# Sliding-window attention and sentence-level experts on one core: the fourth v in one transfer, the fifth v a step earlier, and a conversion behind an output copy

## The chip, the core and the metric

The kernel runs on one core of one Trainium2 chip, in one launch. The metric is the device time of that core in microseconds (us), as the median of the runs shown. The core has a matrix engine (TensorE, PE in the profile), a vector engine (VectorE, DVE), a scalar engine (ScalarE, ACT), a general engine (GpSimd, POOL) and a sync engine (SP) that issues transfers and computes nothing. POOL and SP each feed a queue of the same 16 DMA engines: POOL's queue (q0, "software") carries everything that is converted from float32 on the way, which is q, k and the experts' weights; SP's queue (q1, "hardware") carries v, unconverted, and the outputs.

## What is computed

```python
def _attn_ref(q, k, v):                      # (8, 8, 576, 64) each, float32
    ...
    mask = (rel >= 0) & (rel < window)       # window = 64
    scores = np.where(mask, scores, -1000000000.0)
    ...
    return np.matmul(attn, v)

def _moe_ref(x, w_gate, w1, w2):             # x: (8, 576, 512), the heads side by side
    logits = x.mean(axis=1) @ w_gate
    e_idx = np.argmax(logits, axis=1)        # one of 8 experts for a whole sentence
    ...
    gate_w = probs[np.arange(B), e_idx]
    h = np.maximum(x[mask] @ w1[e], 0.0)     # w1[e]: 512 x 1024
    out[mask] = gate_w[mask, None, None] * (h @ w2[e])   # w2[e]: 1024 x 512
```

Which weights a sentence needs is known only when its attention is finished, its mean is taken and its gate is computed. So the two megabytes of w1 and the two of w2 (float32; half that after conversion) of a sentence can be asked for no earlier than that.

## The kernel before

Eight sentences b of eight heads make 16 units u: unit u holds four heads of sentence u // 2. Of a unit, `load_qk` brings q and k (bf16), `transpose_qk` turns each on PE and ACT or DVE copies it out of PSUM (`leave_qk`), `scores` multiplies them in three chunks c with an exponential on ACT and a mask on DVE (`mask_out`), and `values` multiplies the result (`pt`) with v in two halves, after which DVE normalizes it into `x`. v of a whole sentence comes in one tile `vn` (128 x 36 x 64, float32, 1.2 MB) by `load_v`. `cast_v(u)` converts the half of it that unit u needs: three DVE instructions, one into `va` ("whole") and two from `va` into `vb` ("low" and "high", shifted by 64 rows). `transpose_x` turns x into `xT`, ACT sums it along the way, and `gate(b)` finds the expert. Then `load_w1` and `load_w2` bring its weights. `expert_up` is x times w1, in eight pieces ft (`php`, with the relu to `hT` on ACT), and `expert_down` is h times w2 in five pieces (`pso`; DVE or ACT copies each to an `ob` tile, and SP sends that out).

The order is written out by hand. A prologue brings units 0 to 3 on the way. Then comes a loop over steps t = 4, 5, ...; step t does the scores and values of unit t, and between them a stream of expert pieces (`experts(pace)`) of earlier sentences, to keep PE busy. In each even step `next_gate` computes a gate and asks for weights: sentence 1's at t = 4, sentence 2's at t = 6, and so on. `LAG`, `START = 3` and `per_step` set the pace.

Every PSUM tile comes from one pool of four (`tag="ps"`): a matrix product starts only when the tile it is given has been read out. `vpool` has three tiles, so v of sentence 3 takes the tile of sentence 0, and v of sentence 4 that of sentence 1. `opool` has ten output tiles, two sentences' worth. SP issues its transfers one after another in program order, each when what it waits for is there.

The transfers of v around the change are these. `load_v(2, ...)` is held by a one-element copy on POOL until the first half of sentence 0's w1 has landed. `load_v(3, part=20)` follows and brings 20 of 36 blocks. At the start of t = 5, `load_rest(3, 20, ...)` brings the other 16, held in the same way until the second half of sentence 1's w1 has landed. `load_v(4)` stands at the end of t = 5, and from t = 6 on `load_v` stands in `next_gate` behind `load_w2`.

w1 of sentences 0 and 1 comes in two halves (`w1_parts`), and each half serves four pieces ft: pieces 0 to 3 need the first, 4 to 7 the second.

Of the kernel before, what the change touches and what calls it, by code (L numbers as in the profile page):

```python
# [156 lines left out]
def kernel(  # L157
# [10 lines left out]
    nc = tc.nc  # L168
    B, H, S, D = q.shape
# [7 lines left out]
    NM = H * S // 128  # L177
    scale = 1.0 / float(D) ** 0.5

    def P(ins):  # L180
        tc.keep_in_program_order(ins)
        return ins
# [20 lines left out]
    vv = v.rearrange("b h s d -> b (h s) d").rearrange(  # L203
        "b (m p) d -> b p m d", p=128)
# [3 lines left out]
    def load_qk(u):  # L208
        qn = qkn.tile([128, 2, NT * D], BF16, tag="qn")
        kn = qkn.tile([128, 2, NT * D], BF16, tag="kn")  # L210
        P(nc.gpsimd.dma_start(out=qn, in_=qv[u]))
        if u == 0:
            load_v(0)
        P(nc.gpsimd.dma_start(out=kn, in_=kv[u]))
        qk_tiles[u] = (qn, kn)

    v_tiles = {}

    def load_v(b, behind=None, part=0):
        vn = vpool.tile([128, NM, D], FP32, tag="vn")  # L220
        if behind is None:

            P(nc.gpsimd.memset(vn[:, 0, 0:1], 0.0))
        else:

            P(nc.gpsimd.tensor_copy(out=vn[:, 0, 0:1], in_=behind))
        v_tiles[b] = vn
        if part:
            P(nc.sync.dma_start(out=vn[:, 0:part, :], in_=vv[b][:, 0:part, :]))
        else:  # L230
            P(nc.sync.dma_start(out=vn, in_=vv[b]))

    def load_rest(b, part, behind):
        vn = v_tiles[b]
        P(nc.gpsimd.tensor_copy(out=vn[:, part, 0:1], in_=behind))
        P(nc.sync.dma_start(out=vn[:, part:NM, :], in_=vv[b][:, part:NM, :]))

    HM = NM // 2

# [34 lines left out]
    for (half, e, own) in ((0, 0, True), (1, 0, False), (0, 1, False), (1, 1, True)):  # L274
        sl = par[64 * half:64 * half + 64, e, :]
        if own:

            P(nc.gpsimd.affine_select(
                out=sl, in_=sl, compare_op=ALU.is_ge, fill=OUT, base=0,
                pattern=[[1, 64]], channel_multiplier=-1))  # L280
        else:

            P(nc.gpsimd.affine_select(
                out=sl, in_=sl, compare_op=ALU.is_ge, fill=OUT, base=-1,
                pattern=[[-1, 64]], channel_multiplier=1))
    outside = const.tile([128, 3, 6, 64], BF16)
    for c in range(3):
        P(nc.vector.tensor_copy(
            out=outside[:, c].rearrange("p (g e) w -> p g e w", e=2),
            in_=par[:, None, :, :].broadcast_to([128, 3, 2, 64])))  # L290
# [22 lines left out]
    def cast_part(u, part, eng=None):  # L313
        b, qd = divmod(u, 2)
        i = b % 2
        vn = v_tiles[b]
        lo, hi = qd * HM, qd * HM + HM
        l1 = max(lo, 1)

        src = vn if eng is nc.gpsimd else va[i]  # L320
        eng = eng or nc.vector
        if part == "whole":
            copy_on(eng, va[i][:, lo:hi, 0:D], vn[:, lo:hi, :])
        elif part == "low":
            copy_on(eng, vb[i][0:64, lo:hi, 0:D], src[0:64, lo:hi, 0:D])
        else:
            copy_on(eng, vb[i][64:128, l1:hi, 0:D], src[64:128, l1 - 1:hi - 1, 0:D])

    def cast_v(u):
        for part in ("whole", "low", "high"):  # L330
            cast_part(u, part)
# [70 lines left out]
    def mask_out(u, c):  # L402
        pt = pt_tiles[u, c]
        P(nc.vector.tensor_tensor(  # L404
            out=pt, in0=pt, in1=masks[:, c].rearrange("p s g w -> p s (g w)"),
            op=ALU.mult))
# [92 lines left out]
    def gate(b):  # L499
        gl = psum.tile([128, 2, 512], FP32, tag="ps", name="gl")  # L500
        P(nc.tensor.matmul(out=gl[:, 0, 0:E], lhsT=onesf, rhs=gparts[b],  # L501
                           start=True, stop=True))

        glog = small.tile([128, E], FP32, tag="glog")
        P(nc.vector.tensor_copy(out=glog, in_=gl[:, 0, 0:E]))
        gmx = small.tile([128, 8], FP32, tag="gmx")
        P(nc.vector.max(out=gmx, in_=glog))
        graw = small.tile([128, 8], U32, tag="graw")
        P(nc.vector.max_index(out=graw, in_max=gmx, in_values=glog))
        P(nc.vector.tensor_scalar(out=eidx[:, b, :], in0=graw, scalar1=E - 1,  # L510
                                  scalar2=None, op0=ALU.min))
        gnm = small.tile([128, 1], FP32, tag="gnm")
        P(nc.vector.tensor_scalar(out=gnm, in0=gmx[:, 0:1], scalar1=-1.0 / S,
                                  scalar2=None, op0=ALU.mult))
        gate_in[b] = glog, gnm

        ereg = nc.gpsimd.alloc_register(f"er{b}")
        P(nc.gpsimd.load(ereg, eidx[0:1, b, 0:1]))
        experts_of[b] = ds(nc.gpsimd.snap(ereg, donate=True), 1)
        weights[b] = (wpool.tile([128, KB, F], FP16, tag="w1t", name=f"w1t{b}"),  # L520
                      wpool.tile([128, FB, Dm], FP16, tag="w2t", name=f"w2t{b}"))
# [13 lines left out]
    def w1_parts(b):  # L535
        return weights[b][0].rearrange("p k f -> p (k f)").rearrange(
            "p (h k f) -> p h k f", h=NQ, k=KB)

    def load_w1(b):
        if b < 2:  # L540

            src = w1c[experts_of[b]].squeeze(0)
            for hf in range(NQ):
                P(nc.gpsimd.dma_start(out=w1_parts(b)[:, hf],
                                      in_=src[:, :, ts(hf, F // NQ)]))
        else:
            P(nc.gpsimd.dma_start(  # L547
                out=weights[b][0].rearrange("p (g kl) f -> p g kl f", kl=2),
                in_=w1e[experts_of[b]].squeeze(0)))

    def load_w2(b):
        P(nc.gpsimd.dma_start(
            out=weights[b][1].rearrange("p (g i) d -> p g i d", i=4),
            in_=w2e[experts_of[b]].squeeze(0)))
# [102 lines left out]
    def experts(amount):  # L657

        acc[0] += amount
        while acc[0] > 0.0:  # L660
            nxt = next(stream, None)
            if nxt is None:
                return
            nxt[0]()
            halves[0] = False
            acc[0] -= nxt[1]

            free[0] = nxt[2]

    per_step = (8 * 1.0 + 4 * 1.7 + 0.9) / 2  # L670
    START = 3
# [73 lines left out]
    load_w2(0)  # L745
    load_qk(5)
    load_v(2, w1_parts(0)[:, 0, 0, 0:1])
    load_qk(6)
    load_v(3, part=20)
    for c in range(3):  # L750
        scores(2, c)
        if c == 0:
# [28 lines left out]
    for t in range(START + 1, NU + LAG):  # L781
        pace = per_step / 8.0 * 0.96
        on, prev, ahead = t < NU, START + 1 < t <= NU, t + 1 < NU

        def next_gate():
            b = t // 2 - 1
            gate(b)
            load_w1(b)
            if START + 1 < t < NU - 3:
                load_qk(t + 3)  # L790
            load_w2(b)
            if START + 1 < t and t // 2 + 2 < B:
                load_v(t // 2 + 2)
            if t == START + 1:
                load_qk(7)

        gated = START < t <= NU and t % 2 == 0
        if t % 2 == 1 and t + 3 < NU:
            load_qk(t + 3)
        if t == START + 2:  # L800

            load_rest(3, 20, w1_parts(1)[:, 1, 0, 0:1])
        if prev:
            transpose_x(t - 1)
        if ahead and t > 5 and not gated:
            cast_part(t + 1, "whole")
        if on:
            scores(t, 0, not gated)
            scores(t, 1, not gated)
        if t > START + 1:  # L810
            experts(pace)
        if gated:

            next_gate()
            if on:
                mask_out(t, 0)
                mask_out(t, 1)
        if t == START + 1:
            experts(pace)
        if t == NU:  # L820
            gate_weight(B - 1)
            okc = row_check()
        if ahead and t > 5:
            if gated:
                cast_part(t + 1, "whole")
        experts(pace)
        if on:
            scores(t, 2)
        if gated and on:
            gate_weight(t // 2 - 1)  # L830
        if ahead and t > 5:
            cast_part(t + 1, "low")
            cast_part(t + 1, "high")
        if t == START + 1:
            cast_v(t)
        experts(pace)
        experts(pace)

        if ahead:
            transpose_qk(t + 1, 1, leave=False)  # L840
            leave_qk(t + 1, 1, free[0])

        late = t == START + 1
        if late:
            transpose_qk(t + 1, 0)
        elif on:
            values(t, 0)
        halves[0] = on
        experts(pace)
        experts(pace)  # L850
        if ahead and not late:
            transpose_qk(t + 1, 0)
        if late:
            values(t, 0)
        if on:
            values(t, 1)
        halves[0] = on
        if t in (4, 5):
            cast_v(t + 1)
        if t == START + 2:  # L860
            load_v(4)
        if t == NU:
            row_flag(okc)
        experts(pace)
        experts(pace)
    experts(1e9)


# [35 lines left out]
```

## Time and profile before

| | |
|---|---|
| time, three runs | 225.25, 225.32 and 226.03 us; median 225.32 |
| profiled execution | 225.92 us; span from first to last instruction 224.0 us |
| granted TensorE clock, mean | 0.972 |
| busy in the span | PE 201.1 us (90%), ACT 134.2 (60%), DVE 128.6 (57%), POOL 39.1 (17%) |
| moved by DMA | 45.64 MB, 204 GB/s on average |
| POOL's queue, SP's queue | 26.22 MB and 18.75 MB |

Times in the profile are in us from the span's start. A row of a timeline has the start, the duration, the engine, the line, what was done, and in brackets how long the engine had been idle before and what it is taken to have waited for. Where several waits end together, one of them is named. A row of transfers gives how many, the size of one and the us from issue to landing; for v it shows 0.2 KB, the size of one piece, where the transfer is 1.2 MB. The chain of work is followed back from the last instruction to what released it.

### The profile page before, as it was taken

How to read it: one execution, taken by the hardware profiler on the slowest of the kernel's cores; microseconds unless marked ns; L12 is line 12 of the kernel's file. 1: busy time of each engine (PE TensorE's matmuls, PEld its weight loads, DVE VectorE, ACT ScalarE, POOL GpSimd, SP SyncE). 2: the span in 40 equal slices, each digit the busy share in tenths (PEclk: the TensorE clock that was granted, in tenths of full speed). 3: DMA queues.
4: the chain of work that ended last, by engine and by line, in shares of the span. 5: the costliest groups of instructions: out<-in, count | busy, mean ns of one | idle time of the engine just before them, and what ended most of it. 6: DMA issues, size and time to landing. Idle time of an engine off the chain costs nothing.

```text
span 224.0 us, 6996 instructions
## 1 busy us (share of the span) xinstructions
PE 201.1 (90%) x3012; PEld 141.4 (63%) x3012; DVE 128.6 (57%) x310; ACT 134.2 (60%) x221; POOL 39.1 (17%) x69
## 2 busy tenths in 40 slices
PE   7859759999799897999999999999999998999960
PEld 2437638856586556865696658775777567569520
DVE  2538696557866665576774769395939373330120
ACT  2275695964768464785769476968495656417300
POOL 7170161053000700034000700050002000200000
PEclk9976999999999999999999999999999999999995
DMA  5999899999999999999999999999956990699141
GB/s 69 243 256 246 149 157 219 242 251 235 257 225 203 236 223 244 230 288 217 244 227 277 218 231 235 250 264 219 246 141 113 212 266 5 97 225 263 52 136 41
DMA packets 34310, 45.64 MB, mean 204 GB/s; under 512 B 7136, under 2 KB 26720, under 8 KB 34272
## 3 DMA queue, kind: packets, MB, share of 16 engines
q0 software_dynamic: 14624, 26.22, 65.3%
q1 hardware_dynamic: 18704, 18.75, 28.9%
q8 instruction: 25, 0.41, 0.7%
q10 hardware_dynamic: 944, 0.16, 0.4%
q14 instruction: 13, 0.11, 0.1%
HBM read 61.90 MB, written 9.44 MB: 318 GB/s over the span
## 4 chain that ended last, share of the span: by engine, by line
PE 64%; DMA 12%; ACT 11%; DVE 6%; issue 2%; POOL 1%; POOLq 0%
PE php L570 26%; PE pso L584 20%; DMA w1t<-in_moe_w_dram 8%; PE tp L342 6%; ACT xT L470 5%; DMA kn<-in_k_dram 4%; PE op L425 4%; ACT hT L574 4%; PE sp L382 2%; PE pso L601 2%; ACT pt L397 2%; DVE x L441 1%; PE tp L462 1%; DVE vb L311 1%; PE gl L501 1%
## 5 line engine op out<-in xcount | busy, mean ns | idle before, releaser
L570 PE MATMUL php<-xT,w1t 128*128 128x288 f16 x512 | 70.0, 287 | 3.4 <-DMA w1t<-in_moe_w_dram 2.3
L574 ACT ACTIVATE hT<-php,gatew 128x576 f16<-128x576 f32 x64 | 47.2, 744 | 28.8 <-PE php L570 28.6
L570 PEld LDWEIGHTS <-w1t 128*128 128x128 f16 x512 | 56.0, 115 | 10.0 <-DMA w1t<-in_moe_w_dram 2.9
L584 PE MATMUL pso<-w2t,hT 128*128 128x512 f16 x256 | 60.2, 380 | 0.2
L397 ACT ACTIVATE pt<-sp 128x768 f16<-128x768 f32 x48 | 36.4, 817 | 7.5 <-PE sp L382 7.5
L584 PEld LDWEIGHTS <-hT 128*128 128x128 f16 x256 | 23.3, 98 | 26.1 <-issue 1.2
L311 DVE COPY ob<-pso 128x512 f32<-128x512 f32 x23 | 15.9, 690 | 22.9 <-PE pso L584 22.7
L441 DVE TENSOR_TENSOR x<-op,linv 128x640 f16<-128x640 f32 x32 | 26.4, 825 | 1.1
L404 DVE TENSOR_TENSOR pt<-pt,masks 128x768 f16<-128x768 f16 x42 | 22.6, 554 | 5.7 <-ACT pt L397 4.7
L355 ACT COPY dst<-tp 128x1152 bf16<-128x1152 bf16 x16 | 18.0, 1124 | 11.9 <-PE tp L342 11.7
L547 POOL DMA_DIRECT2D w1t<-in_moe_w_dram x6 | 4.4, 729 | 112.8 <-DVE pt L404 91.5
L470 ACT ACTIVATE xT<-tp 128x576 f16<-128x576 f16 x28 | 17.9, 646 | 9.2 <-PE tp L462 9.2
L425 PE MATMUL op<-vb,pt 128*64 128x65 f16 x320 | 16.2, 198 | 0.8 <-DVE ob L311 0.7
L311 DVE COPY vb<-va 64x1152 f16<-64x1152 f16 (+1 forms) x32 | 15.9, 498 | 0.5
L425 PEld LDWEIGHTS <-pt 128*64 128x64 f16 x640 | 13.9, 114 | 3.3 <-issue 2.4
L425 PE MATMUL op<-va,pt 128*64 128x65 f16 x320 | 15.9, 198 | 0.0
L382 PE MATMUL sp<-dst 64*64 64x128 bf16 (+1 forms) x672 | 14.2, 218 | 1.9 <-ACT dst L309 1.2
L382 PEld LDWEIGHTS <-dst 64*64 64x64 bf16 x672 | 10.3, 110 | 8.7 <-issue 4.5
L311 DVE CAST va<-vn 128x1152 f16<-128x1152 f32 x16 | 12.2, 763 | 6.2 <-DMA vn<-in_v_dram 6.1
L493 DVE SCALAR_TENSOR_TENSOR gpart<-wg,pooled,gpart 128x8 f32<-128x8 f32 x21 | 4.8, 226 | 18.4 <-ACT xT L470 18.1
L342 PE MATMUL tp<-ident,kn 128*64 128x128 bf16 x288 | 11.5, 227 | 1.9 <-DMA kn<-in_k_dram 1.9
L342 PEld LDWEIGHTS <-kn 128*64 128x64 bf16 x288 | 9.0, 113 | 6.0 <-issue 3.5
(74 smaller groups left out, 178.5 us busy)
## 6 DMA issues: line engine op xcount, KB each, us to landing
w2t<-in_moe_w_dram POOLq DMA_DIRECT2D x8, 1024.0 KB, 17.6
out_dram<-ob SPq DMA_DIRECT2D x31, 256.0 KB, 8.1
w1t<-in_moe_w_dram POOLq DMA_DIRECT2D x6, 1024.0 KB, 9.4
qn<-in_q_dram POOLq DMA_DIRECT2D x16, 288.0 KB, 13.2
kn<-in_k_dram POOLq DMA_DIRECT2D x16, 288.0 KB, 14.3
w1t<-in_moe_w_dram POOLq DMA_DIRECT2D x4, 512.0 KB, 8.3
out_dram<-ob SPq DMA_DIRECT2D x16, 64.0 KB, 7.3
vn<-in_v_dram SPq DMA_DIRECT2D x1, 640.0 KB, 21.1
```

What stands on the lines that cost most here:

```text
L311: P(eng.tensor_copy(out=out, in_=in_))
L342: P(nc.tensor.transpose(out=tp[64 * s:64 * s + 64, ts(t, 128)], in_=src[:, s, ts(t, D)], identity=ident, tile_position=(0, 64 * s)))
L355: P(nc.scalar.copy(out=dst.rearrange("p (x r t) -> p x r t", x=2, t=NT), in_=view))
L382: P(nc.tensor.matmul(out=sp[64 * half:64 * half + 64, s, 64 * (qblk - 6 * c):64 * (qblk - 6 * c) + n], lhsT=kT[64 * s:64 * s + 64, ts(kblk ...
L397: P(nc.scalar.activation(out=pt, in_=sp[:, :, 0:384], func=AF.Exp, scale=scale))
L404: P(nc.vector.tensor_tensor(out=pt, in0=pt, in1=masks[:, c].rearrange("p s g w -> p s (g w)"), op=ALU.mult))
L425: P(nc.tensor.matmul(out=op[64 * half:64 * half + 64, xx, 65 * jj:65 * jj + 65], lhsT=pt[:, s, 64 * (g % 6):64 * (g % 6) + 64], rhs=win, s ...
L441: P(nc.vector.tensor_tensor(out=x[:, :, h0 * D:(h0 + 2) * D].rearrange("p j (x c) -> p x j c", x=2), in0=view[:, :, :, 0:64], in1=li[:, :, ...
L470: P(nc.scalar.activation(out=xT[:, kb, :], in_=tp[:, kl, 0:S], func=AF.Copy, accum_out=pooled[:, b, kb:kb + 1]))
L570: P(nc.tensor.matmul(out=php[:, sc, 0:288], lhsT=w1t[:, kb, cols], rhs=xT[:, kb, ts(sc, 288)], start=(kb == 0), stop=(kb == KB - 1)))
L574: P(nc.scalar.activation(out=hT[:, ft].rearrange("p (sc s) -> p sc s", sc=2), in_=php[:, :, 0:288], func=AF.Relu, scale=gatew[:, b:b + 1]))
L584: P(nc.tensor.matmul(out=pso[:, 0, :], lhsT=hT[:, fb, ts(mt, 128)], rhs=w2t[:, fb, :], start=(fb == 0), stop=(fb == FB - 1)))
```

## The change

Four edits go together. v of sentence 3 comes in one transfer of 36 blocks at the place where 20 blocks came before, and `load_rest` with its hold on POOL is gone. v of sentence 4 is asked for in step 4, right behind sentence 1's w2. The conversion of unit 5's half of v stands in step 4 behind two more calls of `experts`. The parameter `part` goes.

```diff
-    def load_v(b, behind=None, part=0):
+    def load_v(b, behind=None):
...
-        if part:
-            P(nc.sync.dma_start(out=vn[:, 0:part, :], in_=vv[b][:, 0:part, :]))
-        else:
-            P(nc.sync.dma_start(out=vn, in_=vv[b]))
-
-    def load_rest(b, part, behind):
-        vn = v_tiles[b]
-        P(nc.gpsimd.tensor_copy(out=vn[:, part, 0:1], in_=behind))
-        P(nc.sync.dma_start(out=vn[:, part:NM, :], in_=vv[b][:, part:NM, :]))
+        P(nc.sync.dma_start(out=vn, in_=vv[b]))
...
-    load_v(3, part=20)
+    load_v(3)
...
-            if START + 1 < t and t // 2 + 2 < B:
+            if t // 2 + 2 < B:
                 load_v(t // 2 + 2)
...
-        if t == START + 2:
-
-            load_rest(3, 20, w1_parts(1)[:, 1, 0, 0:1])
...
-        if t in (4, 5):
+        if t == START + 2:
             cast_v(t + 1)
-        if t == START + 2:
-            load_v(4)
         if t == NU:
             row_flag(okc)
         experts(pace)
         experts(pace)
+        if late:
+
+            cast_v(t + 1)
```

**SP, from v of sentence 2 to v of sentence 5.** `vn_583` is v of sentence 2 and `vn_590` that of sentence 3. Sentence 4's is `vn_1494` before and `vn_1073` after; `vn_1594` is sentence 5's. The `ob` tiles are the five outputs of sentence 0. Before:

```order
L231 DMA vn_583<-in_v_dram 128x36x64 [waits Pool_49]
L229 DMA vn_590<-in_v_dram 128x20x64 [waits DMAHW0_49,Pool_49]
L596 DMA out_0_dram<-ob_1090 128x512 [waits DVE_49]
L596 DMA out_0_dram<-ob_1127 128x512 [waits Activation_49]
L609 DMA out_0_dram<-ob_1181 64x256 [waits DVE_49]
L609 DMA out_0_dram<-ob_1181 64x256 [waits DMAHW1_49]
L596 DMA out_0_dram<-ob_1202 128x512 [waits DMAHW2_49,DVE_49]
L596 DMA out_0_dram<-ob_1264 128x512 [waits DMAHW3_49,DVE_49]
L236 DMA vn_590<-in_v_dram 128x16x64 [waits DMAHW4_49,Pool_49]
L231 DMA vn_1494<-in_v_dram 128x36x64 [waits DMAHW5_49,Pool_49]
```

Now:

```order
L228 DMA vn_583<-in_v_dram 128x36x64 [waits Pool_49]
L228 DMA vn_590<-in_v_dram 128x36x64 [waits DMAHW0_49,Pool_49]
L228 DMA vn_1073<-in_v_dram 128x36x64 [waits DMAHW3_49,Pool_49]
L588 DMA out_0_dram<-ob_1093 128x512 [waits DVE_49]
L588 DMA out_0_dram<-ob_1130 128x512 [waits Activation_49]
L601 DMA out_0_dram<-ob_1184 64x256 [waits DMAHW1_49,DVE_49]
L601 DMA out_0_dram<-ob_1184 64x256 [waits DMAHW2_49]
L588 DMA out_0_dram<-ob_1205 128x512 [waits DVE_49]
L588 DMA out_0_dram<-ob_1264 128x512 [waits DMAHW4_49,DVE_49]
L228 DMA vn_1594<-in_v_dram 128x36x64 [waits DMAHW5_49,Pool_49]
```

Both transfers of 36 blocks now stand ahead of all outputs of sentence 0, where one of 20 blocks stood, and the two that stood behind those outputs are gone. On POOL the one-element write that releases sentence 4's v moves from behind the hold for w1 to right behind sentence 1's w2, ahead of q and k of units 7 and 8.

**DVE, at the end of step 4 and the start of step 5.** `x2` is x of sentence 2, `va0` and `vb0` are the converted v, `ob_1264` is the last output of sentence 0. Before:

```order
L441 TENSOR_TENSOR x2_1213<-op_1237,linv_154 128x2x5x64 [waits DVE_49]
L311 CAST va0_120<-vn_583 128x18x64
L311 COPY vb0_122<-va0_120 64x18x64 [waits DVE_49]
L311 COPY vb0_122<-va0_120 64x18x64
L311 COPY ob_1264<-pso_1263 128x512 [waits PE_49]
L489 TENSOR_SCALAR gpart2_1295<-wg_96,pooled_151 128x8 [waits DMAHW1_49,Activation_49]
```

Now:

```order
L433 TENSOR_TENSOR x2_1216<-op_1240,linv_154 128x2x5x64 [waits DVE_49]
L303 COPY ob_1264<-pso_1263 128x512 [waits PE_49]
L303 CAST va0_120<-vn_583 128x18x64
L303 COPY vb0_122<-va0_120 64x18x64 [waits DVE_49]
L303 COPY vb0_122<-va0_120 64x18x64
L481 TENSOR_SCALAR gpart2_1296<-wg_96,pooled_151 128x8 [waits DMAHW1_49,Activation_49]
```

The output copy stands ahead of the three conversions; what comes before and behind them is the same.

**PE, at the first expert piece of sentence 1, in step 5.** `sp` are the scores of unit 5, `w1t1` is sentence 1's w1, `php` its first product. Before:

```order
L382 LDWEIGHTS dst_1157
L382 MATMUL sp_1316<-dst_1178,dst_1157 64x64
L570 LDWEIGHTS w1t1_1068 [waits PE_49,DMASW1_49]
L570 MATMUL php_1335<-xT1_905,w1t1_1068 128x288 [waits Activation_49]
L570 LDWEIGHTS w1t1_1068
```

Now:

```order
L374 LDWEIGHTS dst_1160
L374 MATMUL sp_1317<-dst_1181,dst_1160 64x64
L562 LDWEIGHTS w1t1_1068 [waits DMASW1_49]
L562 MATMUL php_1336<-xT1_905,w1t1_1068 128x288 [waits DVE_49]
L562 LDWEIGHTS w1t1_1068
```

PE's own order is unchanged, but this product is given another PSUM tile: before it took the one that ACT reads last in `transpose_x`, now it takes the one that DVE empties by the output copy above.

## The prediction

> **What bounds the kernel now.** I read the waits of PE first: PE is busy for 90% of the span, so time is won only where it stands still or starts late.
>
> ```profile
> PE php L570 <- DMA w1t<-in_moe_w_dram: 2.3, 2, 1.4
> ```
>
> 2.3 us in two waits, the longer one 1.4, the largest of PE's waits for a transfer. Next, the timeline of PE, where the brackets show its neighbours.
>
> ```profile
> 57.51 0.54 PE L382 MATMUL sp<-dst 64*64 64x64 bf16 x28
> 59.04 1.14 PE L570 MATMUL php<-xT,w1t 128*128 128x288 f16 x8 [1.00 <-ACT xT L470]
> 60.41 2.15 PE L570 MATMUL php<-xT,w1t 128*128 128x288 f16 x16
> 63.43 2.15 PE L570 MATMUL php<-xT,w1t 128*128 128x288 f16 x16
> 71.40 1.89 PE L584 MATMUL pso<-w2t,hT 128*128 128x512 f16 x8
> 75.34 0.69 PE L342 MATMUL tp<-ident,kn 128*64 128x128 bf16 x18
> 76.78 0.19 PE L425 MATMUL op<-vb,pt 128*64 128x65 f16 x1 [0.75 <-DVE ob L311]
> 85.46 1.17 PE L570 MATMUL php<-xT,w1t 128*128 128x288 f16 x8 [1.45 <-DMA w1t<-in_moe_w_dram]
> ```
>
> Three holes of 1.00, 0.75 and 1.45 us stand in steps 5 and 6, 3.2 us together. The first is the wait for a PSUM tile (ACT reads it), and the third ends when sentence 2's w1 lands. DVE explains the second:
>
> ```profile
> 56.71 0.75 DVE L311 CAST va<-vn 128x1152 f16<-128x1152 f32 x1
> 58.45 0.69 DVE L311 COPY ob<-pso 128x512 f32<-128x512 f32 x1
> 75.28 0.86 DVE L311 CAST va<-vn 128x1152 f16<-128x1152 f32 x1 [1.98 <-DMA vn<-in_v_dram]
> 76.06 0.67 DVE L311 COPY ob<-pso 128x512 f32<-128x512 f32 x1
> ```
>
> At 75.28 DVE had waited 1.98 us for the second piece of the fourth v, and the output copy queued behind that conversion frees the tile that PE wants at 76.78 - 0.75 = 76.03. So the three holes have three causes, and each edit touches one. (Sentences count from 0: the fourth v is sentence 3's, the fifth sentence 4's.)
>
> **DMA.** All 16 engines are full in these steps, so moving v moves weights. These rows are of the transfers issued at 47.24, 48.0, 48.7 and 50.1 (w1 in halves, w2, k of unit 7), then of w1 at 73.40 and of the next sentence's w1:
>
> ```profile
> w1t<-in_moe_w_dram POOLq DMA_DIRECT2D x1, 512.0 KB, 9.0
> w1t<-in_moe_w_dram POOLq DMA_DIRECT2D x1, 512.0 KB, 12.8
> w2t<-in_moe_w_dram POOLq DMA_DIRECT2D x1, 1024.0 KB, 17.9
> kn<-in_k_dram POOLq DMA_DIRECT2D x1, 288.0 KB, 20.2
> w1t<-in_moe_w_dram POOLq DMA_DIRECT2D x1, 1024.0 KB, 12.0
> w1t<-in_moe_w_dram POOLq DMA_DIRECT2D x1, 1024.0 KB, 9.7
> ```
>
> They land at 56.2, 60.8, 66.6 and 70.3; sentence 2's w1 takes 12.0 us where the next one's takes 9.7. Packet counts of stretches say why. In order: 40.5:48 (q and k beside v), 51.9:54 (w1 nearly alone), 57.3:58.3 (w1 beside small outputs), 66:72 (q and k beside the fourth v's second piece), 74.5:77.5, 81.5:83 (w1 beside v), 96.5:98.5 (q and k beside outputs).
>
> ```profile
> q0 software_dynamic: 862, 0.94, 72.5%
> q1 hardware_dynamic: 863, 0.88, 42.2%
> ...
> q0 software_dynamic: 391, 0.40, 115.1%
> ...
> q0 software_dynamic: 132, 0.14, 79.2%
> q1 hardware_dynamic: 125, 0.11, 41.9%
> ...
> q0 software_dynamic: 874, 0.95, 91.3%
> q1 hardware_dynamic: 873, 0.22, 27.7%
> ...
> q1 hardware_dynamic: 642, 0.66, 112.1%
> ...
> q0 software_dynamic: 66, 0.27, 88.6%
> q1 hardware_dynamic: 64, 0.07, 15.7%
> ...
> q0 software_dynamic: 197, 0.21, 62.0%
> q1 hardware_dynamic: 196, 0.33, 52.2%
> ```
>
> Where both queues have work, they go packet for packet (862 to 863, 874 to 873, 66 to 64). The rates are 862/7.5 = 115 pairs/us for q or k with v, 186/us for w1's small packets alone, 132/us in a pair, 44/us for w1's or w2's large packets with v, 98.5/us for q or k with outputs. The split fourth v travels in packets of 0.22 MB/873 = 0.25 KB, the whole ones in 1 KB: 27.7% x 6 us x 16/873 = 30 ns for a quarter of what takes 42.2% x 7.5 x 16/863 = 59 ns. And from 74.5 to 77.5 no packet of POOL's queue moved, though w1 had been asked for at 73.40: the fifth v had the engines alone.
>
> The Trainium skill (DMA: Bandwidth & Descriptors, Bandwidth, why small descriptors are slow) puts the overhead of a 256-byte descriptor at 27%. The trace says more here: 4 x 30 against 59 ns is a factor of two. By the page's figure the one transfer would save about a fifth of the split v's engine time, by the rows half of it, and no term below depends on which.
>
> **Part by part.** *The conversions behind the output copy.* DVE's total is unchanged. The copy starts when x is done, at 56.71, and PSUM is free 1.74 us earlier, so the product at 59.04 may start when the scores end: 57.51 + 0.54 = 58.05, a gain of 1.00 at most. Copy and conversions together end when they did, ahead of unit 5's values. What is late next is ACT:
>
> ```profile
> 58.88 1.51 ACT L397 ACTIVATE pt<-sp 128x768 f16<-128x768 f32 x2
> ```
>
> The second and third products need PSUM tiles that these two exponentials empty, at about 59.65 and 60.4. At 2.15/2 = 1.08 us a product they end at 61.8, and what stands between them and the fourth takes 63.43 - 62.56 = 0.87, so the fourth starts at 62.7 instead of 63.43. I take 0.7, between 0 and 1.00.
>
> *The fourth v whole.* It lands right behind the third instead of at 75.28, so DVE's wait of 1.98 us is gone, and the conversion runs at 73.3, behind the masks. The output copy waits only for its product, which began at 71.40 and took 1.89. PE's 0.75 goes: 0.75. Its next need, the mask of the third chunk, is ready by then, since ACT's exponential does not depend on v. Removing the hold on POOL is worth nothing: POOL idles there.
>
> *The fifth v beside w1.* Up to 51.9 nothing differs for w1's start. Taking the landing of the first half, 56.2, less its 512/186 = 2.75, POOL's queue starts effectively at 53.5. Now every packet of it has a v packet beside it:
>
> - w1: 512/132 = 3.9 for each half, landing at 57.4 and 61.3. The first is needed at 58.05, the second by the fifth product (63.43 + 1.08 = 64.5 before, 63.8 now).
> - w2: 256/44 = 5.8, landing at 67.1; needed at 71.40 - 0.7 = 70.7.
> - q and k of unit 7: 512/115 = 4.4, landing at 71.5; needed at 75.34 - 0.7 = 74.6.
> - q and k of unit 8, beside outputs: 512/98.5 = 5.2, to 76.7.
> - w1 of sentence 2: 256/44 = 5.8, to 82.5.
>
> The v packets suffice about up to unit 7 (1024 + 256 + 512 = 1792 of the 2304 of two v, of which some 500 pass before). PE, freed of the first two holes, is ready for w1 at 85.46 - 1.45 - 1.45 = 82.56. So w1 is just in time, and the hole of 1.45 closes. A second way gives the same: issued at 73.40 - 0.7 and 9.7 us under way, it lands at 82.4. Only lateness counts, and the rates are good to half a us, so I take 0.25 off: 1.2, between 0 and 1.45.
>
> *SP.* It issues in order, and an issue can be held up:
>
> ```profile
> 34.60 11.21 SPq L229 DMA_DIRECT2D vn<-in_v_dram  x1
> 61.66 8.12 SPq L231 DMA_DIRECT2D vn<-in_v_dram  x1
> ```
>
> Behind the fifth v's issue now stand the five outputs of sentence 0, and they will leave some 10 us later. `opool` holds two sentences' outputs, so the next copy that needs one of these tiles is sentence 2's, two steps on: covered, cost 0. Without that cover DVE and ACT, and PE behind them, would wait those 10 us. The sixth v's issue, behind the outputs, has until its conversion in step 9. POOL's one-element write, now ahead of q and k of units 7 and 8, waits only for conversions done in the prologue: hidden.
>
> Sum: 0.7 + 0.75 + 1.2 = 2.65 us off 225.92, so 223.3 for a profiled execution. That execution was 0.6 above the median of 225.32; off the median it is **222.7**. Behind step 6 all waits hang on PE's own progress (sentence 3's w1 lands 9.7 us after an issue that moves with it), so I see nothing that gives it back.
>
> **Rivals.** *The two queues overlap less than I read (slower).* The mechanism is turn-taking: each packet of v, now there from start to end, costs POOL's queue its full time. Place: w1 of sentence 1 to w1 of sentence 2. By the durations, one after the other, in ns/16 for each pair: w1 99 + 59, w2 322 + 59, q or k 101 + 59, with outputs 101 + 85. That is 10.1 + 6.1 + 5.1 + 6.0 + 6.1 = 33.4 us from 53.5, so sentence 2's w1 lands at 86.9 against 85.46: 1.4 slower, 226.7, or 227.3 if w1 also starts as late behind its issue as w1 did at 73.40. It decides as soon as that landing passes 85.5. For it: the queue of POOL got nothing for 3 us while v was alone. Against it: the shares add up to 115% (72.5 + 42.2), so pairs do overlap.
>
> The Trainium skill (DMA: Bandwidth & Descriptors, Queues, rings and completion order) has the engines take turns between queues packet by packet, 9 to 17 descriptors typically. The counts agree on the turns. Taken as strict turns this rule speaks against the change, and gives this rival.
>
> *Sentence 2's w1 keeps its 12.0 us*, because outputs and the sixth v take the fifth's place in front of it. Issued 0.6 earlier it lands at 84.8, and only 0.65 remains: 224.7. Against it: sentence 3's w1 also had outputs beside it, and took 9.7.
>
> *The change doesn't do what it says:* SP holds the fifth v so long that it goes out after w1 as before, and only the first two terms count, 223.9 to 225.3.
>
> **How the numbers follow.** A measurement of this kernel can tell about 0.5%, 1.1 us, from no change: below 224.2 is faster, above 226.4 slower. The forecast has 0.60, with an own range of 222.0 to 224.0 (terms between 1.3 and 3.2). Turn-taking has 0.22, all but a little of it above 226.4. The kept 12 us has 0.13, within 0.5%. The late fifth v has 0.05, half faster. Faster 0.62, same 0.17, slower 0.21. With 222.0 to 226.2, the first, third and fourth case are in, and a little of the second; about 2 in 10 are out.
>
> **What would show it.** PE's waits of 1.00 at 59, 0.75 at 76 and 1.45 at 85 gone; no wait of DVE for v near 75; no packets of 0.25 KB; w1 of sentence 1 landing by 58 and 62, w1 of sentence 2 under 10 us after its issue. I am wrong if a wait of PE for w1, w2 or k appears between 57 and 83, or if sentence 2's w1 lands after 84.

## The result: 0.8% faster, by one of the four edits

The changed kernel takes 223.49 us (median of 15 runs, 222.59 to 226.14) against 225.31 us for the kernel before (15 runs beside it, 224.60 to 226.15). The ratio is 0.9917, with a 95% interval of 0.9894 to 0.9941: 1.8 us less, where 2.65 were forecast. The profiled execution took 225.25 us (span 223.4), 1.76 above the median. Its trace shows one thing that cost it time, the clock behind the last hole below.

The page after, its lines on packets and on SP's queue. The count under 512 B was 7136, the share of the queue 28.9% before:

```profile
DMA packets 30838, 45.64 MB, mean 204 GB/s; under 512 B 2512, under 2 KB 23248, under 8 KB 30800
q1 hardware_dynamic: 15232, 18.75, 27.5%
```

The same bytes in 3472 packets fewer: 4624 of the small ones are gone, which at 0.25 KB is the 1.2 MB of the fourth v.

PE's timeline after: the places of the three holes, and what follows the last. The row at 74.70 is the product that stood at 76.78 before; a row without brackets had no wait.

```profile
57.74 1.17 PE L562 MATMUL php<-xT,w1t 128*128 128x288 f16 x8 [0.17 <-DMA w1t<-in_moe_w_dram]
...
74.70 0.19 PE L417 MATMUL op<-vb,pt 128*64 128x65 f16 x1
...
79.67 1.90 PE L576 MATMUL pso<-w2t,hT 128*128 128x512 f16 x8
83.52 1.96 PE L562 MATMUL php<-xT,w1t 128*128 128x288 f16 x8 [1.95 <-DMA w1t<-in_moe_w_dram]
...
85.88 1.77 PE L562 MATMUL php<-xT,w1t 128*128 128x288 f16 x8
```

The holes of 1.00 and 0.75 are gone (0.17 is left of the first, now a wait for w1). The hole of 1.45 at sentence 2's w1 has not closed, it is 1.95. Eight products of 288 columns take 1.96 and 1.77 behind it, where they took 1.17 before it. The stretches 83.5:85, 85:87 and 87:88 give the granted clock in the column ahead of the last two (1.00 is full speed):

```profile
83.50:85.00 1.50, 1.48 (x7) 1.02 (x8) 0.00 (x0) 0.00 (x0) 0.00 (x0) 0.58 1.16 248
85.00:87.00 2.00, 2.00 (x21) 1.09 (x20) 0.01 (x1) 1.44 (x2) 0.00 (x0) 0.50 1.16 247
87.00:88.00 1.00, 1.00 (x21) 0.69 (x20) 0.99 (x3) 0.32 (x1) 0.00 (x0) 0.92 1.09 235
```

For some 3.4 us behind the hole PE has half its clock. The kernel before had nothing of that here.

DVE's timeline after, the four rows that stood in the prediction:

```profile
56.25 0.69 DVE L303 COPY ob<-pso 128x512 f32<-128x512 f32 x1
56.86 0.75 DVE L303 CAST va<-vn 128x1152 f16<-128x1152 f32 x1
72.04 0.75 DVE L303 CAST va<-vn 128x1152 f16<-128x1152 f32 x1
72.71 0.68 DVE L303 COPY ob<-pso 128x512 f32<-128x512 f32 x1
```

The copy now stands ahead of the first conversion, and the second conversion no longer waits for v.

POOL's issues of w1 for sentences 1, 2 and 3, first before, then after:

```profile
47.24 1.50 POOL L544 DMA_DIRECT2D w1t<-in_moe_w_dram  x2 [12.67 <-DVE pt L404]
73.40 0.72 POOL L547 DMA_DIRECT2D w1t<-in_moe_w_dram  x1 [12.34 <-DVE pt L404]
98.96 0.72 POOL L547 DMA_DIRECT2D w1t<-in_moe_w_dram  x1 [21.19 <-DVE pt L404]
```

```profile
46.77 1.50 POOL L536 DMA_DIRECT2D w1t<-in_moe_w_dram  x2 [12.65 <-DVE pt L396]
72.24 0.71 POOL L539 DMA_DIRECT2D w1t<-in_moe_w_dram  x1 [20.35 <-PE pso L576]
98.45 0.74 POOL L539 DMA_DIRECT2D w1t<-in_moe_w_dram  x1 [21.81 <-DVE pt L396]
```

And of after the us to landing for the two halves of sentence 1's w1, for sentence 2's w1 and for sentence 3's:

```profile
w1t<-in_moe_w_dram POOLq DMA_DIRECT2D x1, 512.0 KB, 10.9
w1t<-in_moe_w_dram POOLq DMA_DIRECT2D x1, 512.0 KB, 14.4
w1t<-in_moe_w_dram POOLq DMA_DIRECT2D x1, 1024.0 KB, 11.2
w1t<-in_moe_w_dram POOLq DMA_DIRECT2D x1, 1024.0 KB, 8.9
```

These rows give three yardsticks, each from the one traced execution of a kernel. They are counted from the issue of sentence 1's w1. The executions differ there already, and not by edit (46.5 to 47.8; two kernels with the whole fourth v have 47.65 and 46.56; after is 0.47 ahead of before). From it on:

- **landing**: when sentence 2's w1 has landed. Before 73.40 + 12.0 - 47.24 = 38.2; after 72.24 + 11.2 - 46.77 = 36.7.
- **ready**: when PE could have used it (its start less its wait). Before 85.46 - 1.45 - 47.24 = 36.8; after 83.52 - 1.95 - 46.77 = 34.8.
- **section**: when sentence 3's w1 is asked for, which needs PE's work of steps 4 to 7. Before 51.7; after 51.7 too: what PE won by 83.5 in this execution went in the half clock. From landing to section it took 15.0 us, where four other kernels with the whole v and a full clock here took 13.5 (in the table below).

### The profile page after: what moved, and what is told of

It reads as the page before. It is cut to its first block, busy times and chain, and to the rows that moved or that the text cites. A ratio compares the mean times of both kernels' runs of the same rounds, so it can differ in the third digit from the quotient of the medians.

```text
span 223.4 us, 6992 instructions
## 1 busy us (share of the span) xinstructions
PE 202.9 (91%) x3012; PEld 142.7 (64%) x3012; DVE 128.6 (58%) x310; ACT 134.0 (60%) x221; POOL 38.7 (17%) x68
## 2 busy tenths in 40 slices
DMA packets 30838, 45.64 MB, mean 204 GB/s; under 512 B 2512, under 2 KB 23248, under 8 KB 30800
## 4 chain that ended last, share of the span: by engine, by line
PE 65%; ACT 12%; DMA 11%; DVE 6%; issue 2%; POOL 1%; POOLq 0%
PE php L562 26%; PE pso L576 21%; DMA w1t<-in_moe_w_dram 7%; PE tp L334 6%; ACT xT L462 5%; ACT hT L566 4%; DMA qn<-in_q_dram 4%; PE op L417 4%; PE sp L374 2%; DVE x L433 2%; ACT pt L389 2%; PE pso L593 2%; PE tp L454 1%; DVE vb L303 1%; PE gl L493 1%
## 5 line engine op out<-in xcount | busy, mean ns | idle before, releaser
L562 PE MATMUL php<-xT,w1t 128*128 128x288 f16 x512 | 71.4, 291 | 2.4 <-DMA w1t<-in_moe_w_dram 2.1
L417 PE MATMUL op<-vb,pt 128*64 128x65 f16 x320 | 15.6, 196 | 0.0
L417 PE MATMUL op<-va,pt 128*64 128x65 f16 x320 | 15.4, 196 | 0.0
L417 PEld LDWEIGHTS <-pt 128*64 128x64 f16 x640 | 13.3, 112 | 2.4 <-issue 1.3
L431 DVE RECIPROCAL linv<-op 128x10 f32<-128x10 f32 x32 | 6.9, 215 | 10.8 <-PE op L417 10.7
```

The lines of the kernel that those rows point to most:

```text
L417: P(nc.tensor.matmul(out=op[64 * half:64 * half + 64, xx, 65 * jj:65 * jj + 65], lhsT=pt[:, s, 64 * (g % 6):64 * (g % 6) + 64], rhs=win, s ...
L562: P(nc.tensor.matmul(out=php[:, sc, 0:288], lhsT=w1t[:, kb, cols], rhs=xT[:, kb, ts(sc, 288)], start=(kb == 0), stop=(kb == KB - 1)))
```

## The experiments

Two theories at the start. *Independent holes*: the prediction's, three causes and three gains that add. *Landing*: sentence 2's w1 arrives when the DMA engines have carried what lies ahead of it, and what PE wins before that moment it waits away there. In the diffs "before" and "changed" say which kernel was edited. Ratios are against the kernel before, run beside each. The groups of runs come from different chips, so kernels are compared by ratio and not by median.

| kernel | median, us | ratio, 95% interval | wait for sentence 2's w1 | landing | section |
|---|---|---|---|---|---|
| before | 225.31 | 1 | 1.45 | 38.2 | 51.7 |
| changed | 223.49 | 0.9917 [0.9894, 0.9941] | 1.95 | 36.7 | 51.7 |
| order only | 225.08 | 0.9975 [0.9946, 1.0004] | 1.53 | 38.0 | 51.5 |
| whole only | 223.81 | 0.9904 [0.9869, 0.9938] | 1.05 | 36.5 | 50.0 |
| early only | 228.24 | 1.0122 [1.0087, 1.0158] | none | 36.0 | 54.7 |
| whole + early | 223.92 | 0.9921 [0.9887, 0.9956] | 0.69 | 36.2 | 49.7 |
| whole + order | 224.08 | 0.9940 [0.9903, 0.9976] | 1.64 | 36.6 | 50.1 |
| two transfers, no hold | 226.44 | 1.0035 [1.0002, 1.0069] | 2.63 | 38.1 | 53.0 |
| halves by partition | 230.04 | 1.0193 [1.0148, 1.0239] | none | 39.1 | 56.1 |
| changed + filler | 223.93 | 0.9915 [0.9889, 0.9942] | 0.53 behind filler | 36.6 | 50.1 |
| changed, q and k behind | 223.96 | 0.9917 [0.9882, 0.9952] | none | 34.6 | 49.7 |
| changed, outputs behind | 221.81 | 0.9845 [0.9799, 0.9891] | none | 34.6 | 48.3 |
| the same, old order | 222.55 | 0.9854 [0.9816, 0.9892] | none | 35.4 | 49.2 |
| the same, late fifth v | 221.74 | 0.9836 [0.9798, 0.9873] | 0.18 | 35.0 | 48.8 |

### One edit at a time

**The order alone.**

```diff
  (before)
-        if t in (4, 5):
+        if t == START + 2:
             cast_v(t + 1)
...
         experts(pace)
         experts(pace)
+        if late:
+            cast_v(t + 1)
```

> The kernel before, with the conversions of unit 5 behind the output copy and nothing else. Theory A (the three holes are independent and add): PE's hole of 1.00 us at 59 shrinks to 0.2 or less, everything behind it moves 0.7 earlier, 224.6 us against 225.3 (ratio 0.997). Theory B (whatever PE wins before sentence 2's w1 is waited away there, because that landing is set by the engines' load): the hole at 59 goes, the wait for w1 near 85 grows from 1.45 to about 2.1, and the time stays within 0.1% of before.

PE's timeline of this kernel at the three holes:

```profile
59.66 2.12 PE L570 MATMUL php<-xT,w1t 128*128 128x288 f16 x16 [0.30 <-ACT pt L397]
...
76.36 0.19 PE L425 MATMUL op<-vb,pt 128*64 128x65 f16 x1 [1.10 <-DVE ob L311]
...
85.13 1.17 PE L570 MATMUL php<-xT,w1t 128*128 128x288 f16 x8 [1.53 <-DMA w1t<-in_moe_w_dram]
```

1.00 has become 0.30, as the prediction's term had it, and what PE waits for there is now ACT's exponential. But the second hole grew from 0.75 to 1.10 and the third from 1.45 to 1.53: both are waits for a transfer, which did not come sooner. 0.7 won, 0.43 waited away, and the time is not distinguished from no change.

**The fourth v whole, alone.**

```diff
  (before)
-    load_v(3, part=20)
+    load_v(3)
...
-        if t == START + 2:
-
-            load_rest(3, 20, w1_parts(1)[:, 1, 0, 0:1])
```

> The kernel before, with the fourth v in one transfer (no second piece, no hold on POOL); the fifth v stays at the end of step 5. Theory A: DVE's wait near 75 and PE's 0.75 us at 76 go, the wait for sentence 2's w1 stays 1.45 or shrinks, because the packets of 0.25 KB are gone: 224.5 us (ratio 0.997). Theory B: PE's 0.75 goes and the wait for w1 grows by as much unless w1 lands earlier; time within 0.1% of before.

```profile
59.45 1.14 PE L570 MATMUL php<-xT,w1t 128*128 128x288 f16 x8 [0.99 <-ACT xT L470]
...
84.19 1.17 PE L570 MATMUL php<-xT,w1t 128*128 128x288 f16 x8 [1.05 <-DMA w1t<-in_moe_w_dram]
```

The 0.75 is gone, and beyond what the term said, sentence 2's w1 lands 1.7 sooner (38.2 to 36.5). The section is 1.7 shorter and the ratio 0.9904: this edit alone has a gain that is not told apart from the whole change's (0.9917).

**The fifth v early, alone.**

```diff
  (before)
-            if START + 1 < t and t // 2 + 2 < B:
+            if t // 2 + 2 < B:
                 load_v(t // 2 + 2)
...
-        if t == START + 2:
-            load_v(4)
```

> The kernel before, with the fifth v asked for behind sentence 1's w2; the fourth v is still split and its second piece held behind w1. Theory A: the wait for w1 of sentence 2 shrinks by 1.2, DVE's wait for the second piece stays or grows (it now stands behind the fifth v and the outputs): 224.1 us, or no gain where the second piece lands later than 75. Theory B: all of the change's gain comes from this edit, 223.5 us (ratio 0.992).

PE, DVE and SP of this kernel:

```profile
79.82 0.19 PE L425 MATMUL op<-vb,pt 128*64 128x65 f16 x1 [3.83 <-DVE ob L311]
```

```profile
78.40 0.76 DVE L311 CAST va<-vn 128x1152 f16<-128x1152 f32 x1 [5.16 <-DMA vn<-in_v_dram]
```

```profile
50.88 13.34 SPq L596 DMA_DIRECT2D out_dram<-ob  x2
...
66.80 0.39 SPq L236 DMA_DIRECT2D vn<-in_v_dram  x1
```

On SP the outputs stand 13.34 us behind the fifth v, and behind them the second piece of the fourth v leaves at 66.80 instead of 61.05. DVE waits 5.16 us for it, PE 3.83, and the kernel is 1.2% slower. The prediction had expected that a delay of the outputs costs nothing. That holds only when no piece of v stands behind them, so this edit needs the whole fourth v. Yet sentence 2's w1 lands 2.2 sooner (38.2 to 36.0), with w1 asked for at the same time as before (73.36 and 73.40). The fifth v goes out at 49.60 here, and in 74.5:77.5 POOL's queue moves 96 packets, where it moved none before: w1 no longer stands behind a fifth v that has the engines alone.

**Whole and early together** (both diffs).

> The changed kernel without the move of the conversions behind the output copy. Theory A: the hole of 1.00 at 59 is back, the rest is as in the changed kernel: 0.5 to 0.7 us slower than the changed kernel, 224.1 (ratio 0.995). Theory B: same as the changed kernel, 223.5 (0.992), with PE's wait for sentence 2's w1 shorter by what the hole at 59 takes, and under 1.4 us.

The landing comes 0.3 sooner than with the whole v alone and the wait shrinks from 1.05 to 0.69, where the prediction had it all but gone. The whole v alone had brought the landing 1.7 sooner and the early v alone 2.2; both together bring 2.0. So these two terms don't add either: they take away the same delay. In time the two are not distinguished (0.9921 and 0.9904).

**Whole and order together.**

> The fourth v whole and the conversions behind the copies of outputs, the fifth v still where it was. Independent holes: the order's 0.7 us comes off the whole transfer's time: about 223.1, TensorE's wait for w1 of sentence 2 near 1.0. Landing theory (w1 of sentence 2 arrives when the engines deliver it, and TensorE waits away whatever it won before): same time as with the whole transfer alone, about 223.8, and the wait for w1 of sentence 2 near 1.7.

```profile
57.85 1.17 PE L570 MATMUL php<-xT,w1t 128*128 128x288 f16 x8 [0.48 <-DMA w1t<-in_moe_w_dram]
...
83.21 1.17 PE L570 MATMUL php<-xT,w1t 128*128 128x288 f16 x8 [1.64 <-DMA w1t<-in_moe_w_dram]
```

The first hole is 0.48 instead of 0.99, and the last 1.64 instead of 1.05. Landing and section are those of the whole v alone (36.6 and 50.1 against 36.5 and 50.0). That is the landing theory: all four kernels with a whole fourth v and none of the order, the early v, both or either, land between 36.2 and 36.7. In these traces independent holes are refuted, and in time this kernel (0.9940) is not faster than the whole v alone (0.9904).

### Why the whole transfer brings sentence 2's w1 sooner

```diff
  (before, without load_rest)
         if part:
             P(nc.sync.dma_start(out=vn[:, 0:part, :], in_=vv[b][:, 0:part, :]))
+            P(nc.sync.dma_start(out=vn[:, part:NM, :], in_=vv[b][:, part:NM, :]))
```

> The kernel before, with the fourth v still in two transfers (20 and 16 blocks) but asked for one right behind the other at the early place, with no hold for the second half of w1. Size theory (the small packets of 0.25 KB keep the other queue back): there are still some 4600 small packets, w1 of sentence 2 lands about as late after w1 of sentence 1 as in the kernel before (38.2 us behind its issue), and only DVE's wait for v (0.75 us of TensorE) goes: about 225.0. Place theory (what helped was that no piece of the fourth v travels late): DVE's wait goes, w1 of sentence 2 lands some 36.5 us behind w1 of sentence 1, TensorE's wait there is near 1.0, and the time is that of the whole transfer, about 223.8.

Nothing is held and no piece travels late, yet the landing is that of the kernel before (38.1). So it was not the hold. SP's issues from 50 on show where it goes, first here, then with the whole v alone:

```profile
50.41 12.40 SPq L597 DMA_DIRECT2D out_dram<-ob  x2
...
66.36 10.78 SPq L232 DMA_DIRECT2D vn<-in_v_dram  x2
```

```profile
49.30 6.22 SPq L596 DMA_DIRECT2D out_dram<-ob  x2
...
60.13 17.56 SPq L231 DMA_DIRECT2D vn<-in_v_dram  x2
```

And the two queues' packets in 74.5:77.5, again here and then with the whole v:

```profile
q1 hardware_dynamic: 640, 0.65, 111.0%
q0 software_dynamic: 2, 0.01, 1.3%
```

```profile
q0 software_dynamic: 301, 0.40, 74.2%
q1 hardware_dynamic: 388, 0.39, 43.4%
```

The queues go packet for packet (before, 874 packets to 873 in 66:72). For each packet of POOL's queue a v in packets of 0.25 KB gets a quarter of the bytes that it gets in packets of 1 KB. It drags on (its second piece lands 26.3 us after its issue at 45.36), the outputs wait behind it on SP for 12.40 us, and the fifth v comes out only at 66.36. POOL's queue meanwhile runs ahead and dry (3 packets in 71:72, against 116 with the whole v). When sentence 2's w1 is asked for at 72.80, the fifth v has the engines to itself: 640 packets to 2. With large packets v is done early, and in the same stretch 301 packets of POOL's queue move. The time that the small packets take on the engines is a small part of it: where v had nearly all of the engines, small packets brought 0.51 MB in 2.5 us (before, 49.5:52), large ones 0.65 MB in 3 us (here, 74.5:77.5), so 0.20 against 0.22 MB/us. PE's hole is 2.63 in this kernel, and the granted clock behind it, in 85:88, is 0.57; the section grows to 53.0.

```profile
85.00:88.00 3.00, 3.00 (x28) 1.83 (x27) 0.17 (x1) 1.44 (x2) 0.00 (x0) 0.57 1.16 246
```

To part the number of transfers from the size of the packets, the fourth v was cut by partitions:

```diff
  (before, without load_rest)
+            P(nc.sync.dma_start(out=vn[0:64], in_=vv[b][0:64]))
+            P(nc.sync.dma_start(out=vn[64:128], in_=vv[b][64:128]))
```

> As the two transfers back to back, but the fourth v is cut by partitions (0 to 63, 64 to 127, all 36 blocks each) and not by blocks. Size theory (what costs is the 0.25 KB packet): if the page counts about 2500 packets under 512 B, the loss is gone though there are still two transfers: w1 of sentence 2 lands some 36.5 us behind the issue of sentence 1's w1, time as with the whole transfer, about 223.8; if it counts some 4600 more small ones or over, it lands at 38 or later and the time is 226 or more. Rival (two transfers cost as such, whatever the packets): large packets, and still 38 us and 225.5 to 226.5.

```profile
DMA packets 34310, 45.64 MB, mean 200 GB/s; under 512 B 7136, under 2 KB 26720, under 8 KB 34272
```

The packets are 0.25 KB again, so the two stay together: every kernel with the v in parts had the small packets, and none with it whole. Which of the two matters is therefore not shown. The landing of 39.1 says little here: DVE waits 5.49 us for this v and PE 4.86 behind it, so sentence 2's w1 is asked for only at 78.04, and it lands 8.2 us later. PE's clock is near 0.5 from 75 to 81, and the time is 230.04. The Trainium skill (DMA: Bandwidth & Descriptors, Rules for kernel authors) advises one transfer over 128 partitions instead of two over halves, since they share the same engines; this run agrees, at 230.04 against 223.81 us. What its trace shows, though, is a v that comes late in small packets.

### Is it the landing?

**q and k of unit 8 behind sentence 2's w1.**

```diff
  (changed)
-        if t % 2 == 1 and t + 3 < NU:
+        if t % 2 == 1 and t + 3 < NU and t != START + 2:
             load_qk(t + 3)
...
             load_w1(b)
+            if t == START + 3:
+                load_qk(8)
```

> The changed kernel, with q and k of unit 8 asked for behind sentence 2's w1 instead of ahead of it. Landing theory (TensorE waits there for what the queue has to deliver ahead of w1, 0.5 MB of it q and k): w1 lands some 4 us earlier, the wait of 1.95 us goes, with it the half clock behind it, and the time falls by 1 to 2.5 us, to 221.0 to 222.5, unless k of unit 8 (lands now at 78) is late for its scores, which would show as a wait of TensorE for k or its transposes after 83. Rival (the time of w1's landing is set by its issue and not by what stands ahead of it): w1 lands as late as before, same time, about 223.5.

w1 lands 2.1 sooner (34.6) and PE no longer waits for it. Then it stands 1.53 us ahead of k of unit 8, which was issued at 74.50 and landed 11.4 later, at 85.9:

```profile
85.94 0.69 PE L334 MATMUL tp<-ident,kn 128*64 128x128 bf16 x18 [1.53 <-DVE vb L303]
```

The page names DVE for that wait, but the time is that of k's landing. What was expected came only as far as its "unless": both loads are needed within 3 us of each other, and changing places only changes which one is late. Sentence 2's w2, now behind q and k, made PE wait another 0.56 at 96.85. The time is that of the changed kernel (ratios 0.9917 and 0.9917).

**The outputs of sentence 0 behind the sixth v.** So something had to go that PE does not need. `expert_down` keeps the issues for sentence 0 in a list:

```diff
  (changed)
-            P(nc.sync.dma_start(out=out[b, ts(mt, 128), :], in_=ob))
+            def leave():
+                P(nc.sync.dma_start(out=out[b, ts(mt, 128), :], in_=ob))
+            leave_or_keep(b, leave)
...
+    def leave_or_keep(b, leave):
+        if b == 0:
+            kept.append(leave)
+        else:
+            leave()
...
             if t // 2 + 2 < B:
                 load_v(t // 2 + 2)
+            if t == START + 3:
+                for leave in kept:
+                    leave()
```

> The changed kernel, with the six output transfers of sentence 0 (1.2 MB) held back to behind the sixth v's issue, so that none of them travels ahead of sentence 2's w1. Landing theory (what the engines have to carry before that w1 sets when it lands, and TensorE waits for it): 1.2 MB at some 240 GB/s is 5 us of the engines; q and k of unit 8 land 3 to 4 us earlier than 75.1 and 77.9, w1 of sentence 2 by about 80.5 instead of 83.45, the wait of 1.95 us goes and with it the half clock behind it, so sentence 3's w1 is issued 1.5 to 3 us earlier behind sentence 1's (51.7 now) and the time falls to 221.0 to 222.3. Rival (the wait comes back behind it, at w2 of sentence 2 or at q and k of unit 9, beside which the outputs now travel): waits of TensorE for these between 86 and 105, time 223 to 225.

```profile
79.94 1.90 PE L583 MATMUL pso<-w2t,hT 128*128 128x512 f16 x8
81.68 1.14 PE L569 MATMUL php<-xT,w1t 128*128 128x288 f16 x8
```

No wait, and 1.14 us for eight products: full clock. The section falls to 48.3 and the time to 221.81 us, ratio 0.9845. Its interval ends at 0.9891 and that of the changed kernel begins at 0.9894, which is close; the two kernels below, which hold the outputs back too, have 0.9854 and 0.9836. k of unit 8 lands 23.2 us after its issue (26.7 in the changed kernel). The rival's effect is there, but small: sentence 3's w1 now travels beside the outputs, lands 11.4 us after its issue instead of 8.9, and PE waits for it once:

```profile
106.81 2.15 PE L569 MATMUL php<-xT,w1t 128*128 128x288 f16 x16 [0.48 <-DMA w1t<-in_moe_w_dram]
```

That is a quarter of the wait that was removed; between 60 and 106 PE has none over 0.32.

**What are the other two edits worth once the landing is out of the way?** The same kernel with the old order, and with the fifth v asked for a step later:

> Outputs of sentence 0 held back as in the last kernel, fourth v whole and fifth v early, but the conversions in their old order, ahead of the copies of outputs. Landing theory (the order's gain is real only where TensorE doesn't wait for sentence 2's w1 behind it): TensorE's wait of 1.0 us near 59 is back, no wait for w1 of sentence 2, and sentence 3's w1 is issued 0.7 to 1.0 us later behind sentence 1's than in the last kernel (48.28): 49.0 to 49.3; time some 0.7 above it, 222.5. Rival (the order is worth nothing anywhere, other work takes the gain): 48.3 and 221.8.

> Outputs of sentence 0 held back, fourth v whole, conversions behind the copies, but the fifth v asked for in the step after, as in the kernel before. Theory that the early fifth v is worth nothing by itself: no wait of TensorE for w1 of sentence 2, sentence 3's w1 48.3 us behind sentence 1's, time 221.8. Rival (the fifth v now lies in front of sentence 2's w1 and takes the engines): a wait of 0.5 to 1.5 us for that w1, 49 to 50 us, time 222.3 to 223.3.

With the old order the hole is back and nothing eats it:

```profile
58.50 1.14 PE L577 MATMUL php<-xT,w1t 128*128 128x288 f16 x8 [0.99 <-ACT xT L477]
```

The section is 49.2, so the order is worth 0.9 us of trace here where it was worth nothing beside the whole v. In time it is not told apart from nothing: the ratios are 0.9854 and 0.9845, which is 0.2 us. With the late fifth v the wait for sentence 2's w1 is 0.18 and the section 0.5 longer, but no difference in time can be told (0.9836 and 0.9845).

### The half clock

```diff
  (changed, first of sentence 2's pieces)
+        if b == 2 and ft == 0:
+            busy(6)
```

> The changed kernel with six dummy products of the kernel's own filler ahead of sentence 2's first product, so that TensorE is busy in the wait for its w1 (no result depends on them). Clock theory (the wait of 1.95 us there lets the clock fall to half for some 3.4 us): no half clock between 83 and 88, the issue of sentence 3's w1 some 1.4 us earlier, and 0.5 to 1.4 us off the changed kernel: about 222.5. Rival (the fall of the clock there is a chance event of the profiled run, or is not caused by the wait): same time as the changed kernel, about 223.5, or up to 0.3 more for the dummies.

```profile
82.47 1.46 PE L671 MATMUL idle<-spin 128*128 128x512 bf16 x5
84.46 1.17 PE L564 MATMUL php<-xT,w1t 128*128 128x288 f16 x8 [0.53 <-DMA w1t<-in_moe_w_dram]
```

With the filler the idle stretch is 0.53, the products take 1.17, and the section is 50.1 instead of 51.7: in the profiled execution the fall of the clock cost about 1.6 us. The median is nonetheless that of the changed kernel (ratios 0.9915 and 0.9917). A reading that fits is that the fall comes in some executions and not in most, and that the profiled one, 1.76 above its median, had it. It is not shown: there is one trace for each kernel. The filler's own profiled execution was 0.95 above its median and that of the whole v alone 1.39 above, both at full clock here, and the mean clocks of the changed kernel's runs don't order its times (0.962 with 225.25 us, 0.984 with 225.21, 0.974 with 222.59).

## Why the prediction was right in the total and wrong in its terms

The time was forecast at 222.7 with a range of 222.0 to 226.2; it is 223.49, and faster, as forecast. The sum of 2.65 is made of three terms, and the runs give each another size. That the total came near is in part luck: two terms were too large and one too small. The direction was right because one of the edits does gain.

- **The order, 0.7.** The hole went as worked out (1.00 to 0.30 when alone, and ACT's exponentials were next). The failed step is that it adds to the others: the next waits are for transfers, which an earlier PE hardly brings sooner (the landing went from 38.2 to 38.0). Beside the whole v it is worth nothing, without the wait behind it 0.9 us of trace.
- **The whole fourth v, 0.75.** Under-sized. Its section gains 1.7 and its ratio is worth some 2.2 us (1.4 to 3.0). The prediction had found the small packets, had weighed what they cost in engine time, and put none of that into the sum. It missed what turn-taking by packets does to the order: small packets keep v, and everything behind it on SP, late. Its "factor of two" (4 x 30 against 59 ns) was measured beside POOL's packets; nearly alone the two sizes moved 0.20 and 0.22 MB/us.
- **The early fifth v, 1.2.** Over-sized: alone it brings the landing 2.2 sooner but costs 2.8 us, since the fourth v's second piece comes late; beside the whole v it brings the landing 0.3 sooner, and in time nothing that can be told. The failed step is the landing. Sentence 2's w1 was to land at 82.5, or 82.0 with the issue 0.47 earlier; it landed at 83.45. The delay starts at the head of the chain: "Up to 51.9 nothing differs for w1's start" was wrong. From 49.5 to 52, with w1 asked for at 46.77, v had the engines nearly alone:

```profile
q1 hardware_dynamic: 534, 0.55, 107.4%
q0 software_dynamic: 13, 0.01, 2.8%
```

  In the kernel before POOL's queue moved 90 packets in that stretch, and 373 in 52:54, where it now moved 167. The halves of sentence 1's w1 landed at 57.7 and 61.9 instead of 56.9 and 60.8, and k of unit 7 at 72.7 instead of 71.0. The prediction had seen this very thing at 74.5 to 77.5 and used it for a rival, not for the sum. And PE was ready at 81.57, not at 82.09: 1.45 late and 0.5 early make the 1.95.

Of the two signs named as showing it wrong, one occurred: between 57 and 83 PE waited for w1, 0.17 us at 57.74, and from 81.57 on it stood in the wait of 1.95. The other did not, though closely: sentence 2's w1 landed half a us short of 84. What was to show it right occurred for the holes of 1.00 and 0.75, for DVE, for the packets and for sentence 1's w1, and failed for the hole of 1.45 and for "under 10 us" (11.2).

Of the rivals, *keeps its 12.0 us* came nearest as a mechanism: other work took the fifth v's place in front of sentence 2's w1, and it said 224.7. The landing theory is that rival with the whole v's gain added. *Turn-taking without overlap* did not come: sentence 2's w1 landed at 83.45 and not at 86.9, and the shares of the two queues still add up to more than 100% (74.2 + 43.4 in the stretch shown with the whole v alone). *SP holds the fifth v* did not come: it was issued at 49.17, and the outputs behind it stood 14.18 us, and nothing waited for their tiles, as worked out. What they did cost is that they then travelled ahead of sentence 2's w1.

## What to carry to other kernels

Before gains at several holes are added up, find the last one that waits for a transfer: until that transfer's landing is moved, what is won ahead of it becomes a longer wait there. A landing is moved by taking away what travels ahead of it and is not needed yet (here outputs, some 1.6 us beyond the change by the ratios), not by exchanging two loads that are needed at the same time. And read the size of packets on the page as a matter of order, not only of cost: where two queues take turns by packets, the one with small packets falls behind, and all that stands behind it.

## What was not expected of the hardware

**Packets.** The same tile goes in packets of 1 KB when one transfer takes it whole, and of 0.25 KB when it is cut into 20 and 16 blocks or into two halves of 64 partitions (7136 against 2512 packets under 512 B).

**The clock.** The wait of 1.95 us was followed by about 3.4 us at half clock, and those of 2.63 (0.57 in 85:88), 3.83 (the early v alone) and 4.86 (the halves by partition) by a clock near half too; waits of 1.05, 1.45, 1.53 and 1.64 in this place were not. Each is one wait in one trace, so where the limit lies between 1.64 and 1.95, and whether it stays there, is not shown. For the early v alone the stretch behind its 3.83:

```profile
80.00:83.00 3.00, 2.92 (x53) 2.81 (x48) 2.58 (x7) 0.00 (x0) 0.00 (x0) 0.56 1.05 222
```

The Trainium skill (TensorE: Matmul & The Clock Gate, Why this matters for your kernels) warns of idle gaps above about 3 us. Here a wait of 1.95 was followed by the fall, with PE busy on both sides, and by the filler's section it cost about 1.6 us.
